# Fused attention, routing and mixture of experts: a new order of steps, memory products in row tiles, gates in a tensor of their own, more warming matmuls

## Chip, cores and metric

One core of one Trainium2 chip. The metric is the device time of one execution in microseconds (us); less is better.

## What is computed

```python
B, H, S, D = 4, 8, 576, 64
scores = causal(q @ k.T / sqrt(D));  local = softmax(scores) @ v
q_p = phi(q)                                   # elu(q) + 1
mem_out = (q_p @ M_prev) / (q_p @ z_prev + 1e-6)
g = sigmoid(beta)                              # one per head
x = concat_heads(g * mem_out + (1 - g) * local)   # 2304 tokens x 512
logits = x @ w_gate;  e = argmax(logits)          # 8 experts
gate = softmax(logits)[e] * sigmoid(x @ w_output_gate)[e]
out[t] = gate[t] * (relu(x[t] @ w1[e]) @ w2[e])   # 512 -> 1024 -> 512
```

All inputs and the output are float32.

## The kernel before

**Attention.** A pair is two heads of one batch; there are 16 pairs, each cut into five tiles of queries (128, 128, 128, 128, 64 rows). Per tile TensorE makes the scores as sums of three products of split operands, for the two heads on the two halves of the array's rows (L497; the tile of 64 rows at L484). VectorE adds the mask and takes the maximum in one pass into `st` (L555, L523), ScalarE takes the exponential (L560, L532), TensorE turns the probabilities (`pt`, L572, L541), ScalarE or VectorE copies them to SBUF (`PT`, L419), and TensorE multiplies them with the values (`po`, L607). Queries and keys arrive in one tile `qk`; a copy on ScalarE or VectorE makes its high part `hi` (L388), GpSimd the low part `lo` (L392, 1216 elements per partition). GpSimd also starts `phi` (L440), ScalarE and VectorE finish it (L444, L447).

**Memory.** For each batch and tile of queries `memory` multiplies `phi` with `mz`, which holds the matrices of two heads, their products with the gate weights and their norms, 81 columns per head (`me`, L658). VectorE then makes the norm `nr` (L664, L665), scales to `x` (L671) and sums the logits (L674). `combine` turns the attention output, weighs it on VectorE, adds it on GpSimd (`xd`, L729) and stores rows of 513 floats in the DRAM tensor `xs`: 512 of the token and one for its gate.

**Routing.** Per batch, VectorE adds the logits' parts (`lg`, L774), then takes maximum, difference `dl` (L229), one-hot `oha` (L239), `wt` (L254), and the gate `og` (L257 to L272), which SP stores into the last column of `xs` (L275). TensorE ranks the tokens per expert (`rank`), VectorE turns ranks into positions (`pcol`, L280 to L289), GpSimd makes selection matrices `selp` (L305). After the last batch two sums of small matmuls (`pp`, L977) give the row numbers of 25 slots of 128 tokens (`rowi`, L982).

**Order.** Up to the end of attention each engine's work is a list of named steps (`job`); the string `ORDER` of 1154 names sets in which order they are issued, so each engine runs its share of them in that order and waits in place. `RT1_1` is the second routing step of batch 1 (`dl`), `R9` the `lo` of pair 9, `SEL` a `selp`, `ME` a memory product; `:DVE` or `:ACT` says which of two engines copies. VectorE is DVE, ScalarE ACT, GpSimd POOL, and SyncE (SP) issues most DMAs.

**Experts.** 23 slots of up to 128 tokens run one after the other: `gather` fetches rows of `xs` (`xr`, L1033) with GpSimd's indirect DMA, `stage_x` turns and splits them (`xh`, `xl`, L1060), `gemm1` (`h`, L1083) and `gemm2` (`py`) multiply with split weights `whi`, `wlo` made from `raw` (L941, L944), `stage_h` turns and splits in between (L1106 to L1111). ScalarE scales the result by the gate, which came as element 512 of the row, and GpSimd scatters it (L1134).

**Warming.** `warm(n)` issues n matmuls of ones that nobody reads, 12 at the start, 8 and 11 in the last routing, and 11 behind `pp` (L162); their PSUM tile is one of the two buffers of tag `m` that all small products share.

## Time and profile before

| | |
|---|---|
| median of 3 runs | 526.43 us (526.43 to 528.64) |
| the profiled execution | 526.39 us, span 524.4 us |
| busy: TensorE, VectorE, ScalarE, GpSimd | 503.0, 340.9, 279.1, 291.1 us |
| largest lines of the chain that ended last | `h` 23%, `py` 22%, `pt` 7%, `po` 7%, `s` 6%, `me` 4% |
| moved | 68.22 MB, mean 130 GB/s |

The span goes from the first to the last instruction; the time of the execution is 2.0 us longer. A busy TensorE is not one at its peak, since a matmul counts as busy while it waits inside the pipeline. The chain is followed back from the last instruction, at each step to what released it. In bracketed parts of rows, "idle before" is how long the engine stood before this instruction, and what ended that.

### The profile page before, as it was taken

The numbers are of one execution on the slowest core, as the hardware profiler recorded it, in microseconds if no ns is written. First come the engines' busy times: TensorE is split into PE (matmuls) and PEld (weight loads), VectorE is DVE, ScalarE is ACT, GpSimd is POOL, SyncE is SP. The second block draws the span as 40 slices with busy tenths as digits, with TensorE's granted clock in tenths as the row PEclk, the third lists the DMA queues.
The fourth block names the chain that finished last, engine by engine and source line by source line (L and its number), as shares of the span: only waits on it lengthen the run. The fifth ranks groups of instructions, "written<-read, shape, count | busy, mean of one in ns | idle before, by whom it ended". The sixth has DMA issues, their size and how long they took to land.

```text
span 524.4 us, 10513 instructions
## 1 busy us (share of the span) xinstructions
PE 503.0 (96%) x3238; PEld 402.2 (77%) x3238; DVE 340.9 (65%) x821; ACT 279.1 (53%) x643; POOL 291.1 (56%) x264
## 2 busy tenths in 40 slices
PE   8999999999899999688999999999999999999994
PEld 4788778787777887366888888888888888888884
DVE  5998899999689988659898289500073891025600
ACT  5997788696677864353444333333444433343341
POOL 8882584676355223743577657644455675445342
PEclk9999999999699999889999999999999999999998
DMA  7632155263202513396777367511153675115000
GB/s 247 218 133 101 52 166 160 79 190 100 85 26 77 133 57 91 63 326 228 213 242 225 130 191 216 189 40 48 53 147 114 202 221 160 40 44 158 8 3 27
DMA packets 29079, 68.22 MB, mean 130 GB/s; under 512 B 6176, under 2 KB 6688, under 8 KB 29026
## 3 DMA queue, kind: packets, MB, share of 16 engines
q1 hardware_dynamic: 25186, 56.63, 35.3%
q0 software_dynamic: 3696, 10.77, 5.9%
q8 instruction: 32, 0.52, 0.4%
q14 instruction: 21, 0.17, 0.1%
q10 hardware_dynamic: 144, 0.13, 0.1%
HBM read 58.06 MB, written 10.76 MB: 131 GB/s over the span
## 4 chain that ended last, share of the span: by engine, by line
PE 84%; DVE 8%; POOL 3%; issue 3%; ACT 1%; POOLq 0%; DVEq 0%; ACTq 0%
PE h L1083 23%; PE py L1083 22%; PE pt L572 7%; PE po L607 7%; PE s L497 6%; PE me L658 4%; PE hp L1106 3%; PE sd L484 2%; DVE wlo L944 2%; PE px L1052 2%; PE pt L541 2%; PE pv L721 1%; POOL selp L305 1%; DVE st L555 1%; PE pl L824 1%
## 5 line engine op out<-in xcount | busy, mean ns | idle before, releaser
L941 DVE CAST whi<-raw 128x1024 fp32r<-128x1024 f32 x56 | 56.2, 1004 | 119.4 <-ACTq L1090 109.2
L1111 POOL TENSOR_TENSOR hl<-hT,hh 128x512 fp32r<-128x512 f32 x46 | 68.4, 1507 | 87.4 <-ACT hh L1110 87.4
L944 DVE TENSOR_TENSOR wlo<-raw,whi 128x1024 fp32r<-128x1024 f32 x63 | 95.0, 1508 | 4.0 <-ACT whi L941 1.1
L1083 PE MATMUL py<-whi,hh 128*128 (+1 forms) x192 | 77.8, 405 | 1.6 <-DVEq L947 1.6
L560 ACT ACTIVATE st<-st,nm 128x384 f32<-128x384 f32 (+3 forms) x128 | 71.2, 558 | 14.2 <-DVE nm L555 13.7
L1083 PE MATMUL py<-wlo,hh 128*128 (+1 forms) x192 | 74.2, 386 | 0.0
L1083 PE MATMUL py<-whi,hl 128*128 (+1 forms) x192 | 73.9, 385 | 0.0
L1083 PE MATMUL h<-whi,xh 128*128 (+1 forms) x184 | 73.9, 401 | 0.0
L1083 PE MATMUL h<-wlo,xh 128*128 (+1 forms) x184 | 73.0, 397 | 0.0
L1083 PE MATMUL h<-whi,xl 128*128 (+1 forms) x184 | 72.7, 395 | 0.0
L555 DVE CUSTOM_DVE_ANT_0 st<-s,mask 128x128 f32<-128x128 f32 (+3 forms) x128 | 57.9, 483 | 8.4 <-PE s L497 5.3
L1096 ACT ACTIVATE h<-h 128x1024 f32<-128x1024 f32 x23 | 23.6, 1026 | 73.4 <-PE h L1083 73.4
L392 POOL TENSOR_TENSOR lo<-qk,hi 128x1216 fp32r<-128x1216 f32 x15 | 43.1, 2870 | 27.7 <-ACT hi L388 21.3
L1110 ACT CAST hh<-hp 128x512 fp32r<-128x512 f32 x46 | 27.5, 598 | 48.7 <-PE py L1083 48.7
L419 ACT COPY PT<-pt 128x512 f32<-128x512 f32 (+2 forms) x84 | 42.1, 516 | 17.9 <-PE pt L572 14.5
L572 PE MATMUL pt<-ident,st 128*128 128x128 f32 x320 | 47.9, 281 | 3.2 <-ACT PT L419 2.4
L1060 POOL TENSOR_TENSOR xl<-x,xh 128x512 fp32r<-128x512 f32 x22 | 32.4, 1472 | 33.3 <-ACT x L1059 30.1
L1109 ACT COPY hT<-hp 128x512 f32<-128x512 f32 x46 | 27.2, 590 | 42.5 <-PE hp L1106 42.5
L607 PE MATMUL po<-PT,v 128*64 128x320 f32 (+4 forms) x480 | 47.8, 348 | 0.5 <-DVE oT L419 0.4
L572 PEld LDWEIGHTS pt<-ident,st 128*128 128x128 f32 x320 | 36.7, 143 | 9.7 <-ACT PT L419 4.1
L607 PEld LDWEIGHTS po<-PT,v 128*64 128x64 f32 x480 | 30.0, 137 | 18.4 <-issue 3.2
L1083 PEld LDWEIGHTS py<-whi,hh 128*128 128x128 f32 x192 | 36.2, 188 | 8.3 <-DVEq L947 2.2
(199 smaller groups left out, 998.6 us busy)
## 6 DMA issues: line engine op xcount, KB each, us to landing
raw<-in_w SPq DMA_DIRECT2D x64, 512.0 KB, 4.1
qk<-in_qk SPq DMA_DIRECT2D x15, 640.0 KB, 4.2
v<-in_vd SPq DMA_DIRECT2D x16, 320.0 KB, 3.8
xs<-xd SPq DMA_DIRECT2D x12, 256.0 KB, 3.5
...
```

Source lines behind the costliest of these rows:

```text
L392: G.tensor_tensor(c["lo"][:, TQ:], c["raw"][:, TQ:], f32(c["hi"])[:, TQ:], op=ALU.subtract)
L419: (A.copy if e == "ACT" else V.tensor_copy)(dst(), src())
L497: T.matmul(c()["ss", q][j], l[r, lc], m[r, KC:KC + w], start=(a == 0), stop=(a == 2))
L555: V.tensor_tensor_reduce(st[:, :w], c()["ss", qt][j], mask[:, 512 - w:512], -SCALE, 3.0e38, ALU.add, ALU.min, negm()[:, i:i + 1])
L560: A.activation(st, st, AF.Exp, bias=c()["negm"][:, i:i + 1], scale=-1.0, accum_out=sums()[:, qt, 2 * p + j:2 * p + j + 1])
L572: T.transpose(pt[:, (m * k1 + i) * P:(m * k1 + i + 1) * P], st[:, i * P:(i + 1) * P], ident)
L607: T.matmul(po[64 * j:64 * j + 64, qs - q0:q1 - q0], vt[:, k, 64 * j:64 * j + 64], PT[:, j, k, qs:q1], start=(k == 0), stop=(k == kn - 1))
L941: join((A.copy if eng is A else eng.tensor_copy)(whi[:, e % 2, c, :], raws[e, c]))
L944: join(eng.tensor_tensor(wlo[:, e % 2, c, :], raws.pop((e, c)), f32(whi[:, e % 2, c, :]), op=ALU.subtract))
L1060: G.tensor_tensor(xl, x32, f32(xh), op=ALU.subtract)
L1083: i = T.matmul(o[n % nh], l[:, z], m[:, n * 512 + part.start:n * 512 + part.stop], start=(c == 0 and k == 0 and n < nh), stop=(c == 3 and ...
L1111: G.tensor_tensor(hl[:, z], hT[:, z], f32(hh)[:, z], op=ALU.subtract)
```

## The change

The order string is replaced as a whole; the names in it are the same. Gates get a DRAM tensor `gd` of their own, and rows in `xs` are 512 floats; each slot fetches its gates with an indirect DMA of its own (`gather_gate`), right behind its row gather, but for the first three slots, where the three stand behind the last weight split ahead of the first expert product. The memory product works on 64 rows at a time, one head each, with the even heads in one PSUM tile and the odd ones in the other. From the last routing on the warming matmuls have a PSUM pool `pw` of two buffers, and the last group of them is 22 instead of 11.

```diff
--- before.py
+++ after.py
@@ -28,7 +28,6 @@
 HW = D + 16
-XW = DM + 1
...
@@ -43,62 +42,62 @@
 ORDER = """
...
-RT1_1 E10_2_1 F113 M10_2_0 E10_3_0 P9_256_0 P9_0_0 P9_256_1 O9_0:ACT T10_3_0 T10_2_1 O9_256:ACT F213 RT1_2 RT1_3 RT1_4 E10_2_0 M10_3_1 RX1 ME2_1
...
+V10_1:ACT RT1_1 G2_0 N12_3 RT1_2 OUT1_2 T9_4 N22_3 SS10_2 V9_4_0:ACT Tgate40 M10_2_0 RT1_3 M10_2_1 V9_4_1:ACT Tpos20 TS9_0 SS10_3 P9_256_0 M10_3_0
...
@@ -130,7 +129,8 @@
     dpool = ctx.enter_context(tc.tile_pool(name="dram", bufs=1, space=bass.MemoryType.DRAM))
-    xs = dpool.tile([NT + 65, XW], F32, name="xs")
+    xs = dpool.tile([NT + 65, DM], F32, name="xs")
+    gd = dpool.tile([NT + 65, 1], F32, name="gd")
     rx = ctx.enter_context(ExitStack())
@@ -156,7 +156,7 @@
     def warm(n):
-        w = psm.tile([P, 512], F32, name=f"warm{fin.setdefault('w', 0)}", tag="m")
+        w = fin.get("pw", psm).tile([P, 512], F32, name=f"warm{fin.setdefault('w', 0)}", tag="m")
         fin["w"] += 1
@@ -272,7 +272,7 @@
         def gate7():
-            SY.dma_start(xs[row(b, 0):row(b, NQ), DM:XW].rearrange("(t p) c -> p (t c)", p=P), t["og"])
+            SY.dma_start(gd[row(b, 0):row(b, NQ)].rearrange("(t p) c -> p (t c)", p=P), t["og"])
 
@@ -355,7 +355,7 @@
         b, p = divmod(g, NP)
-        c = pr[g] = {"st": {}, "pt": {}}
+        c = pr.setdefault(g, {"st": {}, "pt": {}})
         c["raw"] = (ld if g % 3 == 2 else kq).tile([P, QK], F32, name=f"qk{g}", tag="qk", bufs=1 if g % 3 == 2 else 2)
@@ -368,7 +368,7 @@
         b, p = divmod(g, NP)
-        pr[g]["vt"] = ld.tile([P, NQ, P], F32, name=f"v{g}", tag="v", bufs=3)
+        pr.setdefault(g, {"st": {}, "pt": {}})["vt"] = ld.tile([P, NQ, P], F32, name=f"v{g}", tag="v", bufs=3)
         SY.dma_start(pr[g]["vt"], vd[b, p])
@@ -643,20 +643,21 @@
         r = ROWS[qt]
-        qz = slice(TQ + qt * P, TQ + qt * P + P) if qt < NQ - 1 else slice(0, TQ)
+        qz = slice(TQ + qt * P, TQ + qt * P + P) if qt < NQ - 1 else slice(0, P)
         m = f"{b}_{qt}"
-        zs = [slice(4 * hf, 4 * hf + 4) for hf in range(2)]
+        zs = [slice(j, H, 2) for j in range(2)]
         mes = []
...
                 G.memset(t["lg"], 0.0)
-            for hf in range(2):
-                me = psm.tile([P, 324], F32, name=f"me{m}_{hf}", tag="m")
-                for pp in range(2):
-                    T.matmul(me[:r, 162 * pp:162 * pp + 162], t["phi"][2 * hf + pp][:, qz], t["mz"][:, 2 * hf + pp, :], start=True, stop=True)
-                mes.append(me[:r].rearrange("p (h c) -> p h c", c=81))
+            me = [psm.tile([P, 324], F32, name=f"me{m}_{j}", tag="m") for j in range(2)]
+            for p in range(NP):
+                for j in range(2):
+                    z = slice(64 * j, 64 * j + 64)
+                    T.matmul(me[j][:, 81 * p:81 * p + 81], t["phi"][p][z, qz], t["mz"][z, p, 81 * j:81 * j + 81], start=True, stop=True)
+            mes.extend(x[:r].rearrange("p (h c) -> p h c", c=81) for x in me)
 
@@ -674,7 +675,7 @@
         gs = range(NP * b, NP * b + NP)
-        job(f"ME{m}", "PE", 1085, due + DUE["ME"], product, after=[f"F2{g}" for g in gs] + [f"MC{b}"] + ([f"Y{b - 1}_{qt}"] if b else []) + held(due + HOLD["ME"]), takes=[("m", (m, 0)), ("m", (m, 1))], uses=[("phi", g) for g in gs] + [("mz", b)], mode="F")
+        job(f"ME{m}", "PE", 850, due + DUE["ME"], product, after=[f"F2{g}" for g in gs] + [f"MC{b}"] + ([f"Y{b - 1}_{qt}"] if b else []) + held(due + HOLD["ME"]), takes=[("m", (m, 0)), ("m", (m, 1))], uses=[("phi", g) for g in gs] + [("mz", b)], mode="R")
         job(f"N1{m}", "DVE", 460, due + DUE["N1"], norm, after=[f"ME{m}", "gates2"], takes=[("nr", m)], uses=[("m", (m, 0)), ("m", (m, 1))])
@@ -729,7 +730,7 @@
         def stored():
-            SY.dma_start(xs[row(b, qt):row(b, qt) + r, :DM], o["xd"][:r].rearrange("p h c -> p (h c)"))
+            SY.dma_start(xs[row(b, qt):row(b, qt) + r], o["xd"][:r].rearrange("p h c -> p (h c)"))
 
@@ -843,7 +844,7 @@
         def stored():
-            SY.dma_start(xs[row(b, qt):row(b, qt) + r, :DM], t["xd"][qt][:r].rearrange("p h d -> p (h d)"))
+            SY.dma_start(xs[row(b, qt):row(b, qt) + r], t["xd"][qt][:r].rearrange("p h d -> p (h d)"))
 
@@ -874,7 +875,7 @@
     constants()
-    SY.dma_start(xs[MID:MID + 1, :DM], maskd[0:1, :DM])
+    SY.dma_start(xs[MID:MID + 1], maskd[0:1, :DM])
     for b in range(B):
@@ -946,6 +947,7 @@
 
+    fin["pw"] = rx.enter_context(tc.tile_pool(name="pw", bufs=2, space=PSUM))
     warm(8)
@@ -989,7 +991,7 @@
 
-    warm(11)
+    warm(22)
     V.tensor_tensor(ge, sidx.unsqueeze(2).to_broadcast([P, NSLOT, E]), en[:, 1:].unsqueeze(1).to_broadcast([P, NSLOT, E]), op=ALU.is_ge)
@@ -1028,10 +1030,16 @@
 
+    def gather_gate(s):
+        g = st[s]["g"] = mk.tile([P, 1], F32, name=f"g{s}", tag="g", bufs=4)
+        G.indirect_dma_start(out=g, out_offset=None, in_=gd[:NT + 1], in_offset=bass.IndirectOffsetOnAxis(ap=rowi[:, s:s + 1], axis=0))
+
     def gather(s):
-        xr = mk.tile([P, XW], F32, name=f"xr{s}", tag="xr", bufs=4)
+        xr = mk.tile([P, DM], F32, name=f"xr{s}", tag="xr", bufs=4)
         G.indirect_dma_start(out=xr, out_offset=None, in_=xs[:NT + 1], in_offset=bass.IndirectOffsetOnAxis(ap=rowi[:, s:s + 1], axis=0))
         st[s] = {"x": xr, "ring": s < NMAIN}
+        if s > 2:
+            gather_gate(s)
 
@@ -1115,7 +1123,7 @@
         y = st[s]["y"] = mk.tile([P, DM], F32, name=f"y{s}", tag="y", bufs=2)
-        A.activation(y, py, AF.Copy, scale=st[s]["x"][:, DM:DM + 1])
+        A.activation(y, py, AF.Copy, scale=st[s]["g"])
         done(s, sem_2)
@@ -1123,7 +1131,7 @@
             y = mk.tile([P, 256], F32, name=f"y{s}_{n}", tag="y", bufs=2)
-            A.activation(y, py, AF.Copy, scale=st[s]["x"][:, DM:DM + 1])
+            A.activation(y, py, AF.Copy, scale=st[s]["g"])
             i = G.indirect_dma_start(out=out.rearrange("t (a d) -> (t a) d", a=2), out_offset=bass.IndirectOffsetOnAxis(ap=endi[:, n:n + 1], axis=0), in_=y, in_offset=None, bounds_check=2 * NT - 1, oob_is_err=False)
@@ -1153,6 +1161,8 @@
     ready()
+    for s in range(3):
+        gather_gate(s)
     V.tensor_copy(skip[0:1, 0:1], f32(wlo)[0:1, 0, 3, 0:1])
```

**Where instructions stand.** TensorE, the first memory product of batch 0 (`me` the product, `pt` turned probabilities, `s` and `sd` scores), before:

```order
L541 MATMUL pt_4_669<-ident,st_4_567 128x128 x4
L543 MATMUL pte_4_674<-ident,st_4_567 64x128
L658 MATMUL me_0_0_681<-mz_184,phi_223 128x162
L658 MATMUL me_0_0_681<-mz_184,phi_225 128x162
L658 MATMUL me_0_1_684<-mz_184,phi_397 128x162
L658 MATMUL me_0_1_684<-mz_184,phi_448 128x162
L572 MATMUL pt_0_0_687<-ident,st_0_0_628 128x128
```

and after the change:

```order
L497 MATMUL s_2_0_667<-hi_457 128x384
L497 MATMUL s_2_1_668<-hi_457 128x384
L659 MATMUL me_0_0_678<-mz_185,phi_268 128x81
L659 MATMUL me_0_1_679<-mz_185,phi_268 128x81
L659 MATMUL me_0_0_678<-mz_185,phi_246 128x81
L659 MATMUL me_0_1_679<-mz_185,phi_246 128x81
L659 MATMUL me_0_0_678<-mz_185,phi_343 128x81
L659 MATMUL me_0_1_679<-mz_185,phi_343 128x81
L659 MATMUL me_0_0_678<-mz_185,phi_461 128x81
L659 MATMUL me_0_1_679<-mz_185,phi_461 128x81
L484 MATMUL sd_4_0_689<-lo_458,hi_457 128x288
```

Four matmuls over all rows have become eight that alternate between the two halves, and here they stand behind scores, which also work on halves.

VectorE around `dl` of batch 1 (L229; the rows named ISA are the maxima of scores, `phi` the end of a `phi`, `nr` and `x` a memory product's norm and scaling), before:

```order
L555 ISA st_3_0_2089,nm_1928<-s_3_0_2073,mask 128x512
L555 ISA nm_1928 128x1
L229 TENSOR_TENSOR dl_2091<-lg_1310,mx_2026 128x40
L555 ISA st_2_0_2095,nm_1928<-s_2_0_2063,mask 128x384
L555 ISA nm_1928 128x1
L447 SCALAR_TENSOR_TENSOR phi_1771<-qk_1563,phi_1771 128x576
L233 SCALAR_TENSOR_TENSOR wt_2126<-dl_2091,edesc 128x40
L236 TENSOR_REDUCE mx_2026<-wt_2126 128x5
L239 SCALAR_TENSOR_TENSOR oha<-mx_2026,wt_2126 128x40
L555 ISA st_3_1_2131,nm_1928<-s_3_1_2074,mask 128x512
```

and after the change:

```order
L419 COPY oT_2072<-po_0_2051 128x256
L225 TENSOR_REDUCE mx_2074<-lg_1342 128x5
L419 COPY PT_100<-pt_0_0_2064 128x2x128
L229 TENSOR_TENSOR dl_2091<-lg_1342,mx_2074 128x40
L675 TENSOR_REDUCE lg_1883<-x_0_1927 128x16
L665 SCALAR_TENSOR_TENSOR nr_3_2094<-me_3_0_2079,gt 128x4
L665 SCALAR_TENSOR_TENSOR nr_3_2094<-me_3_1_2080,gt 128x4
L666 RECIPROCAL nr_3_2094<-nr_3_2094 128x8
L233 SCALAR_TENSOR_TENSOR wt_2098<-dl_2091,edesc 128x40
L672 TENSOR_TENSOR x_3_2108<-me_3_0_2079,nr_3_2094 128x4x80
```

`dl` has moved from between two maxima of scores to a place among a memory product's small steps.

VectorE at the end of attention (`lg` the last sums of logits, `pos` to `pcol` the positions of batch 2), before:

```order
L836 TENSOR_REDUCE lg_2730<-yl_1_3249 128x16
L836 TENSOR_REDUCE lg_2730<-yl_1_3255 128x16
L280 TENSOR_TENSOR pos_3268<-rk_3258,oha 128x40
L283 TENSOR_REDUCE ps_3269<-pos_3268 128x5
L286 TENSOR_SCALAR ohe<-ps_3269 128x5
L289 TENSOR_TENSOR pcol<-ps_3269,ohe 128x5
L811 CAST cntb<-cnt 128x8
```

and after the change:

```order
L280 TENSOR_TENSOR pos_3347<-rk_3340,oha 128x40
L283 TENSOR_REDUCE ps_3348<-pos_3347 128x5
L286 TENSOR_SCALAR ohe<-ps_3348 128x5
L289 TENSOR_TENSOR pcol<-ps_3348,ohe 128x5
L837 TENSOR_REDUCE lg_2790<-yl_1_3337 128x16
L812 CAST cntb<-cnt 128x8
L837 TENSOR_REDUCE lg_2790<-yl_1_3329 128x16
```

The two sums have moved behind the positions. GpSimd from the last selections to slot 3, after the change (before, the rows with `gd` are missing and a row of `xr` is 513 long):

```order
L305 TENSOR_SCALAR selp<-pidx,pcol,tokv 128x128 x6
L1039 DMA xr_3563<-xs,rowi 128x512
L329 MEMSET raw_0_3565 1x1
L1039 DMA xr_3570<-xs,rowi 128x512
L1039 DMA xr_3572<-xs,rowi 128x512
L945 TENSOR_TENSOR wlo<-raw_3_3219,whi 128x1024
L1035 DMA g_3598<-gd,rowi 128x1
L1035 DMA g_3600<-gd,rowi 128x1
L1035 DMA g_3602<-gd,rowi 128x1
L1068 TENSOR_TENSOR xl_3637<-x_1_3639,xh_3636 128x512
L1039 DMA xr_3692<-xs,rowi 128x512
L1035 DMA g_3694<-gd,rowi 128x1
```

The first three gate gathers stand behind the weight split of the first expert, the later ones behind their row gather. The memset waits for the store of the last gates, since its tile lies where `og` lay; the first row gather no longer does.

## Rows read from the trace of the kernel before

**Rows 1.** Busy time by stretch: start:end, length, busy of engines (instructions), TensorE clock, DMA share, GB/s.

```profile
8.00:98.00 90.00, 89.68 (x789) 71.70 (x791) 82.89 (x293) 78.85 (x223) 60.53 (x50) 1.00 0.44 148
...
125.40:132.60 7.20, 4.90 (x45) 4.02 (x41) 7.06 (x17) 4.16 (x12) 3.52 (x3) 1.00 0.21 60
132.60:142.80 10.20, 10.12 (x52) 8.64 (x52) 5.93 (x27) 6.56 (x19) 4.10 (x5) 0.50 0.19 70
...
247.10:515.00 267.90, 267.90 (x1296) 219.60 (x1297) 131.90 (x104) 103.20 (x171) 148.97 (x106) 1.00 0.43 132
```

(The engines of a row are PE, PEld, DVE, ACT, POOL, in this order.)

**Rows 2.** The chain of waits, attention: start, us, what.

```profile
70.11 0.87 PE pt L572 x8
...
86.59 1.10 PE me L658 x8
```

**Rows 3.** Timeline of GpSimd, VectorE and TensorE, and one group of VectorE's line 229.

```profile
124.64 1.56 POOL L305 TENSOR_SCALAR selp<-pidx,pcol,tokv 128x128 f16<-128x128 f16 x2
...
125.40 3.58 DVE L229 TENSOR_TENSOR dl<-lg,mx 128x40 f32<-128x40 f32 x1
...
126.17 2.75 POOL L392 TENSOR_TENSOR lo<-qk,hi 128x1216 fp32r<-128x1216 f32 x1
...
132.68 1.75 PE L572 MATMUL pt<-ident,st 128*128 128x128 f32 x7 [2.38 <-ACT PT L419]
...
L229 DVE TENSOR_TENSOR dl<-lg,mx x4: 181/196/3579, 87.1 to 209.8; 128x40 f32<-128x40 f32 x4
...
167.44 2.16 DVE L774 TENSOR_TENSOR lg<-lg,lsum 128x64 f32<-128x64 f32 x2
...
171.47 0.55 PE L572 MATMUL pt<-ident,st 128*128 128x128 f32 x3 [0.64 <-ACT st L560]
```

(The line of the group has the least, median and greatest duration in ns.)

**Rows 4.** Timeline of TensorE's weight loads, scores of 64 rows.

```profile
80.07 0.19 PEld L497 LDWEIGHTS s<-hi,lo 64*128 64x128 f32 x2
80.18 0.19 PEld L497 LDWEIGHTS s<-hi 64*128 64x128 f32 x2
```

**Rows 5.** Timeline of TensorE's matmuls, from transposes to scores.

```profile
79.08 0.60 PE L572 MATMUL pt<-ident,st 128*128 128x128 f32 x4
79.61 0.39 PE L497 MATMUL s<-lo,hi 64*128 64x256 f32 x2
```

**Rows 6.** Timeline from the last routing to the first slot; the landing of gate stores.

```profile
208.37 0.48 DVE L836 TENSOR_REDUCE lg<-yl 128x16 f32<-128x80 f32 x2
...
212.75 0.37 SPq L275 DMA_DIRECT2D xs<-og  x1
...
DMA to landing us min/median/max: 4.5/4.6/4.7
...
216.01 0.16 DVE L982 TENSOR_SCALAR rowi<-pp 128x4 int32<-128x4 f32 x1 [1.55 <-PE pp L977]
...
217.42 4.22 PE L162 MATMUL warm<-ones 128*128 128x512 bf16 x11 [0.93 <-DVE skip L988]
...
218.74 1.59 POOL L1033 DMA_INDIRECT xr<-xs,rowi  x1 [3.00 <-DVE endi L1010]
...
225.02 0.45 PE L1042 MATMUL px_x<-ident,xr 128*128 128x128 f32 x1 [3.38 <-issue]
```

**Rows 7.** The chain of waits, first expert products.

```profile
226.11 3.91 PE h L1083 x12
...
232.55 1.48 DVE wlo L944
...
261.30 5.60 PE h L1083 x24
```

**Rows 8.** GpSimd's gathers as a group; timeline of the tightest slot.

```profile
L1033 POOL DMA_INDIRECT xr<-xs,rowi x23 | 32.5, 1412 | 6.5 <-DVE endi L1010 3.0 <-issue 1.4
...
269.48 2.27 POOL L1060 TENSOR_TENSOR xl<-x,xh 128x512 fp32r<-128x512 f32 x1
...
273.89 0.39 PE L1083 MATMUL h<-whi,xl 128*128 x1
```

(A group's row has its instructions, busy us, mean ns of one, and idle time before them.)

More of the change, by code (lines that the diff above doesn't have):

```diff
@@ new lines @@
+E2_1_0 V1_4_1:ACT F13 R3 M1_3_1 M2_2_0 T2_0 gates E1_3_1 M1_3_0 E2_2_0 load5 load_v3 V2_0:DVE TS1_0 O1_0:DVE MW1 T2_1 MC1 TS0_0 SS2_4 V2_1:ACT T1_3_1
+T2_2_0 M2_2_1 E1_3_0 M2_4_0 V1_3_1:ACT SS2_3 gates2 E2_2_1 V2_2_0:DVE M2_4_1 F14 M2_3_1 M2_3_0 TS0_1 TS1_1 C4:DVE F24 T1_3_0 F23 T2_2_1 V1_3_0:ACT
+V2_2_1:ACT R4 E2_3_1 E2_3_0 E2_4 SS3_1 M3_0_0 M3_1_0 P1_256_0 T2_3_1 V2_3_1:ACT T2_3_0 P1_256_1 V2_3_0:ACT M3_1_1 E3_1_1 E3_0_0 O1_256:DVE E3_1_0 T2_4
+M3_0_1 SS3_2 V2_4_0:DVE ME0_0 E3_0_1 SS3_4 T3_0 V2_4_1:ACT M3_2_0 M3_2_1 C5:DVE R5 E3_2_1 E3_2_0 N10_0 T3_1 TS2_1 SS4_1 M3_4_0 V3_0:ACT V3_1:ACT
@@ new lines @@
+Tpos30 G2_3 R13 M10_4_0 Tpos40 E10_3_1 C14:ACT ME2_1 M10_4_1 N12_1 SS11_1 TS9_1 T10_3_0 load_v12 SS11_4 M11_0_0 N22_1 M11_1_1 M11_0_1 SEL0_3
+V10_2_0:ACT SEL0_1 T10_3_1 MW3 V10_3_0:ACT E10_4 M11_1_0 V10_3_1:ACT E11_0_1 RX1 Tgate11 RK1 E11_0_0 E11_1_1 T10_4 M11_4_0 SS11_2 E11_1_0 load12
+Tpos11 MC3 M11_4_1 TS10_1 R14 V10_4_0:DVE ME2_4 V10_4_1:DVE OUT1_4 T11_0 T11_1 M11_2_0 N12_4 E11_4 V11_0:ACT Tgate31 Tgate21 SS11_3 V11_1:ACT T11_4
+E11_2_0 F115 N22_4 GA1 M11_3_0 P11_0_0 P10_256_0 V11_4_0:DVE M11_3_1 Tpos21 F215 M11_2_1 E11_3_0 O11_0:ACT V11_4_1:ACT P10_0_0 P10_256_1 C12:ACT R12
@@ new lines @@
+E15_0_1 Tgate22 SEL1_0 M15_1_0 CB1 T15_4 E14_2_0 G3_0 O14_0:DVE W3_0 M14_2_1 E15_1_0 O13_256:ACT M15_1_1 V15_4_0:ACT PLl4_0 PLl1_0 fetch1 E15_1_1
+YLl4_0 T15_0 V15_0:ACT V15_4_1:DVE TL4_0 YLl1_0 XLl4_0 E14_2_1 GA2 PLl0_0 T14_2_0 YLl0_0 XLl0_0 W3_1_0 G3_1 CJ2 fetch2 V14_2_0:ACT T15_1 V15_1:ACT
+Tgate42 TS15_0 ME3_3 TL0_0 SS15_3 SS15_2 N13_3 T14_2_1 SEL0_4 N23_3 XLl1_0 TS15_1 V14_2_1:ACT M15_2_1 P15_0_0 O15_0:ACT M15_3_1 Tgate52 P15_512_0
+W3_1_1 TL1_0 M15_2_0 O15_512:ACT E15_2_1 M15_3_0 W3_1_4 E15_2_0 G3_3 Tgate62 fetch3 P14_256_0 P15_128_0 P14_256_1 E15_3_0 E15_3_1 T15_2_0 T15_3_0
@@ L102 @@
+O14_256:DVE O15_128:DVE PLl2_0 V15_2_0:DVE G3_2 PLl1_1 V15_3_0:ACT GO2 T15_3_1 YLl2_0 V15_3_1:ACT YLl1_1 XLl2_0 PLl4_1 TL2_0 XLl1_1 PLl3_0 TL1_1 OL1
+YLl4_1 YLl3_0 XLl4_1 TL4_1 T15_2_1 PLl0_1 YLl0_1 XLl3_0 V15_2_1:ACT W3_1_3 TL0_1 TL3_0 XLl0_1 P15_384_0 P15_256_0 W3_1_2 O15_384:ACT PLl3_1
+O15_256:ACT YLl3_1 PLl2_1 OL0 XLl3_1 YLl2_1 RK2 Tpos12 Tpos22 XLl2_1 Tpos32 Tpos42 SEL2_2 SEL2_1 SEL2_0 SEL2_4 SEL2_3 OL4 OL3 OL2 TL2_1 CB2 TL3_1
 """.split()
```

95 lines of the change are left out of this document (40 added, 55 removed).

## The prediction

> **What bounds the kernel now.** I read the busy time and granted clock by stage first. From 8.00 to 98.00 us TensorE is busy 89.68 of 90 us and VectorE 82.89 [rows 1]: attention is paced by TensorE, with VectorE at 92% close behind. TensorE's "busy" includes queueing inside its pipeline, so I checked it against the spacing of starts: eight transposes take 0.87 us of the chain, 0.109 each [rows 2], and they do run back to back. The reader should therefore expect almost any TensorE time taken out of attention to come back whole, as long as VectorE keeps up. From 247.10 us to the end TensorE is busy 267.90 of 267.90 us at full clock [rows 1]: the expert stage is bound by its own matmuls, which the change does not touch.
>
> Two stretches break the pattern. From 125.40 to 132.60 us TensorE works 4.90 of 7.20 us, and from 132.60 to 142.80 the granted clock is 0.50, the lower of its two levels [rows 1]: TensorE had idled and then ran at half speed for 10.2 us, which cost 5.1. The bridge between the attention and the expert stage (about 207 to 247 us) is a chain over VectorE, GpSimd, a gather and the first expert's matmuls.
>
> The timeline shows what caused the first stretch. VectorE's `dl` (L229), a subtraction of 40 elements with both operands in SBUF, took 3.58 us from 125.40 [rows 3], while its median over four is 196 ns. It ended at 128.98, 0.06 after GpSimd's `lo` (126.17 + 2.75 = 128.92), which had followed `selp` (from 124.64, 1.56) without a pause. So a two-operand SBUF instruction of VectorE stands still until GpSimd pauses. Everything behind it on VectorE came late, then ScalarE's copies of transposed probabilities, and TensorE waited 2.38 us for one. At 167.44 the two `lg` additions (L774) of 64 and 16 elements took 2.16 us together, and TensorE then waited 0.64 [rows 3].
>
> **The change, part by part**
>
> *Memory products in row tiles.* One of the 20 products was four program matmuls of 162 columns over 128 rows, eight in the trace, and takes 1.10 us of the chain [rows 2], 0.138 each. Now it is eight of 81 columns over 64 rows, sixteen in the trace, in pairs on the two halves of the array. The nearest rows are the scores, also pairs of 64 rows: the weight loads of two successive pairs start at 80.07 and 80.18 [rows 4], so a pair takes 0.11 whatever it multiplies, and its two loads run together. Eight pairs cost 0.88, and 20 x (1.10 - 0.88) = 4.4 us go. The lower bound of the new product is its matmuls alone, 8 x 0.138/2 = 0.55; the upper is 16 loads one after another, 1.76. I take 0.88 because the score rows have the same shape of weights.
>
> A change of tile shape costs time: four transposes start 0.109 apart from 79.08, the last at 79.41, and the score behind it starts at 79.61 [rows 5], 0.20 instead of 0.11. The order has 131 stretches of equal tile shape before the routing's end and 146 after the change, so 15 x 0.095 = 1.4 us come back. The Trainium skill (TensorEngine Tiling (Array Packing), Key Properties) says that a change of tiling mode drains TensorE, which speaks against a product that no longer shares the transposes' shape; the page has no price for it, rows 5 have 0.095 us. Net: **-3.0 us**.
>
> *The order.* All 1154 steps are the same, placed otherwise; VectorE has 54 of the 184 copies that either it or ScalarE can do, before and after. What matters is where the routing's two-operand steps stand against GpSimd's long ones. `dl` of batch 1 now stands among the norms of a memory product instead of between two score maxima, and what it delays first is that product's scaling. If the two waits that rows show go, 2.4 + 5.1 + 0.6 = 8.1 us go with them. Bounds: nothing gained (other steps collide instead) and all 8.1, plus little that is spread thinly. The order alone does not say which steps meet, and VectorE's share is still about 90%, so I keep 1.6 back for new collisions: **-6.5 us**. SP's queue is passed too: the gate stores of earlier batches now stand ahead of the last five row stores, where the one that stood among them used to hold the queue.
>
> *Gates apart.* A row is 2048 instead of 2052 bytes, a norm reads every second head: nothing for either, the element counts are the same. The first gather started at 218.74 although its row numbers were written at 216.01 + 0.16 = 216.17. The store of the last gates into the same DRAM tensor was issued at 212.75 and lands 4.5 to 4.7 us later, at 217.45 by the longest [rows 6]. From there to the gather 1.29 us are GpSimd's own start. Without that wait the gather starts 1.29 after 216.17, at 217.46: 1.28 earlier. Also, the order now takes the rank positions of batch 2 before the last two sums of `lg`, which took 0.48 [rows 6]; the selection, the slot numbers and the gather all hang on those positions. Together 1.8 us; below, nothing; above, 2.1, if GpSimd's start is partly done while it waits. The memset and the two gathers behind it still wait for the gates' store, which no longer waits for an earlier gate store and lands by then.
>
> *More warming matmuls, from PSUM of their own.* The 11 matmuls waited 0.93 us for VectorE's `skip` and took 4.22, 0.384 each, mostly at the lower clock; TensorE then idled until 225.02 [rows 6] and began the first expert product at the lower clock too: 12 matmuls took 3.91 us [rows 7], where 24 take 5.60 at full clock, 2.80 for 12. With 22 matmuls that need not wait, from 217.42 - 0.93 - 0.48 = 216.0 on, TensorE is at work for 22 x 0.384 = 8.4 us if the clock is down throughout and half of that if it is up, until 224.4 or 220.2. The first gather lands at 225.02 - 1.8 = 223.2. So the end is either in time or 1.2 late. I take a rise in between, and the 12 matmuls at full clock: 1.1 us. They are on the path: ScalarE's cast of the second expert's weights and VectorE's `wlo` at 232.55 [rows 7] come behind them, and from there VectorE's weight splitting runs to 247.1. Gather and clock: **-2.9 us**, between -0.6 and -3.2.
>
> *Gate gathers.* Each slot gets one more indirect DMA on GpSimd, at the 1412 ns of the row gathers or less [rows 8]. It stands ahead of the scatter and of `xl` of a later slot. In the tightest slot `xl` ended at 269.48 + 2.27 = 271.75, and TensorE used it at 273.89: 2.14 us of cover. A gather at its mean, with a start of 0.3, is covered by that: **0**. If the cover went, each slot that is short would cost the difference. The three that come before are issued behind GpSimd's last weight split and ahead of `xl` of slot 1, and take 3 x 1.4 of the time in which GpSimd waits for that slot's rows.
>
> **The sum.** The profiled execution took 526.39 us, the median of the runs shown is 526.43. 526.39 - 3.0 - 6.5 - 2.9 = **514.0 us**. About 0.5% (2.6 us) is what a measurement of this kernel can tell from no change.
>
> **The rivals**
>
> *A. The waits move.* The order removes these collisions and makes others of the same weight. For it: VectorE stays at about 90% while TensorE has no slack, and both waits that rows show reached TensorE. Against it: after the change the routing steps stand in clusters away from GpSimd's long instructions. Then the second term is 0, and 514.0 + 6.5 = **520.5**.
>
> *B. Slower: more episodes of a late VectorE and a fallen clock.* One wait of 3.6 us cost 2.4 of idling and 5.1 of half clock, 7.5 together. This decides by their number: with two where there was one, 526.39 - 3.0 - 2.9 + 7.5 = 528.0, within 0.5%; with three, **535.5**. For it: one such wait was enough before. Against it: of the two waits that rows show only one did it, the other cost 0.6.
>
> *C. The product halves.* If its weight loads overlap better than the scores', the product takes its matmuls' 0.55: 20 x 0.55 - 1.4 = 9.6 instead of 3.0, and 514.0 - 6.6 = **507.4**. Against it: in rows 4 the loads pace the narrow pairs. The Trainium skill (TensorEngine Tiling (Array Packing), Theoretical Speedup) gives up to two times for a contraction of 64 rows; it would be this case, and rows 4 show the loads as the nearer limit.
>
> *D. The gate gathers reach TensorE.* If one takes the 2.1 us that cover `xl` and half a microsecond more, in six slots like that one, that is 3 us: **517.0**.
>
> **How the numbers follow.** Forecast 0.55, A 0.25, B 0.10, C 0.05, D 0.05. The predicted time is that of the forecast, 514.0. Its own range is 510.5 (all 8.1 us of waits, the gather's 2.1) to 518 (half of the order's term, the gather's lower bound). The range that should hold the time takes in A with 2 us more, and leaves out B and C: 509.5 to 522.5. Faster by over 0.5% (below 523.8): the forecast, C, D and 0.18 of A, 0.83. Within 0.5%: the rest of A and B's mild form, 0.10. Slower: B's hard form, 0.07.
>
> **What would show it.** The products: 16 trace matmuls each, pairs 0.11 apart, some 0.9 us of the chain. The order: `dl`, `wt` and `lg` all near 0.2 us, no stretch of half clock between 10 us and the end of attention, attention ending some 9.5 us earlier. The gates: the first gather within 1.5 us of its row numbers. The warming: full clock when the first expert product begins, and 2.8 us for its first 12 matmuls. The expert stage: 267.9 us as before. The prediction is wrong if attention ends less than 5 us earlier, if a half-clock stretch stands in it, or if an `h` matmul waits for `xl`.

## The result, and the profile after

The changed kernel takes **534.18 us** (median; 526.71 for the kernel before beside it), ratio 1.013 with a 95% interval of 1.0097 to 1.0162. It is slower by some 7 us; the forecast was 514.0. The execution profiled took 534.79 us with a span of 533.1, against 526.39 and 524.4 before: 8.7 us of span to account for.

The stages first. The row numbers of the last routing are written at 217.96 us (before at 216.01, [rows 6]), so attention and routing lost 2 us instead of gaining 9.5. From there to the first transposes of the first expert's rows (`px_x`) it takes 11.73 us, before 9.01. From there to the first `py` it takes 16.2 us, before 14.9. The expert stage is what it was, 276.67 us from the first `py` to the last in both traces. Behind the last `py` come 10.5 us, before 7.8. So 2.0 + 2.7 + 1.3 + 2.7 us make up the 8.7. The busy time by stretch (length, then PE, PEld, DVE, ACT, POOL, the clock, DMA share, GB/s) answers to [rows 1]:

```profile
135.00:140.00 5.00, 3.51 (x39) 2.80 (x39) 4.95 (x15) 2.89 (x12) 2.61 (x1) 1.00 0.10 39
140.00:143.50 3.50, 3.50 (x16) 2.42 (x15) 2.31 (x11) 2.30 (x7) 0.00 (x0) 0.51 0.00 0
...
253.00:523.00 270.00, 269.82 (x1310) 221.45 (x1310) 134.97 (x104) 103.30 (x172) 168.33 (x125) 1.00 0.43 132
...
225.40:235.60 10.20, 5.91 (x16) 4.74 (x17) 4.17 (x8) 2.86 (x6) 8.51 (x6) 0.50 0.89 295
```

The stretch of half clock in attention is shorter (3.4 us instead of 10.2), but the bridge has one of 10.2 us. The timeline of the changed kernel shows why, and what became of the VectorE steps of [rows 3] (start, us, engine, line, operation, in brackets the idle time before and what ended it):

```profile
129.18 2.79 POOL L392 TENSOR_TENSOR lo<-qk,hi 128x1216 fp32r<-128x1216 f32 x1 [8.05 <-issue]
...
129.27 2.73 DVE L286 TENSOR_SCALAR ohe<-ps 128x5 f32<-128x5 f32 x1
...
134.82 2.79 POOL L392 TENSOR_TENSOR lo<-qk,hi 128x1216 fp32r<-128x1216 f32 x1
...
135.46 2.21 DVE L254 TENSOR_TENSOR wt<-lg,oha 128x40 f32<-128x40 f32 x1
...
154.44 0.39 SPq L275 DMA_DIRECT2D gd<-og  x1
...
166.37 1.27 POOL L730 TENSOR_TENSOR xd<-x,y 128x512 f32<-128x512 f32 x1 [4.57 <-DMA xs<-xd]
...
167.67 1.29 DVE L726 TENSOR_TENSOR y<-pv,rr 128x512 f32<-128x512 f32 x2 [1.26 <-POOL xd L730]
...
168.41 0.76 PE L607 MATMUL po<-PT,v 128*64 128x256 f32 x6 [1.16 <-DVE y L726]
...
214.94 0.37 SPq L275 DMA_DIRECT2D gd<-og  x1
...
217.96 0.16 DVE L984 TENSOR_SCALAR rowi<-pp 128x4 int32<-128x4 f32 x1 [0.78 <-PE pp L979]
...
218.29 4.91 PE L162 MATMUL warm<-ones 128*128 128x512 bf16 x22
...
219.11 1.23 POOL L1039 DMA_INDIRECT xr<-xs,rowi  x1 [1.42 <-issue]
225.24 0.09 POOL L329 MEMSET raw<- 1x1 f32 x1 [4.90 <-issue]
...
229.69 0.45 PE L1050 MATMUL px_x<-ident,xr 128*128 128x128 f32 x1 [6.49 <-issue]
```

Three things are to be read here. First, `dl` is short now, but `ohe` and `wt` are caught by GpSimd's `lo` in its place: each starts just behind a `lo` and ends 0.03 to 0.06 us after it. Second, GpSimd's `xd` stood 4.57 us until an earlier store of rows had landed, VectorE's `y` then waited 1.26 for `xd`, and TensorE 1.16 for `y`; this begins behind the gates' store of 154.44. Third, the first gather starts 1.15 us after its row numbers, as the prediction wanted, but its rows reach TensorE only 10.6 us later (before 6.3, [rows 6]), and the memset in front of the second gather, which needs the buffer that this store reads, does not run until 10.3 us after the gates' store was issued (the row names no releaser). TensorE, done with its 22 warming matmuls, idles and falls to half clock; the chain has 5.17 us for the first 12 `h`, before 3.91 [rows 7].

The view of the DMA queues from 216 to 226 us (packets, MB, their time as a share of 16 engines) says what the gather ran into:

```profile
q0 software_dynamic: 21, 0.09, 53.7%
q8 instruction: 1, 0.02, 2.1%
```

The 21 packets of the gathers kept their engines for 53.7% of 160 us, 4.1 us each, and even the fetch of program code by another queue took 3.4. The gates' store itself is 640 elements of 4 bytes, now side by side in `gd`; before they were 2052 bytes apart. The store's own packets don't show the difference. In the 2.1 us from its issue on, its queue (q1) has 656 packets of 7.4 ns each, and as many of 7.5 ns in the run with 64 bytes that comes next; only the packets of others behind it are long:

```profile
q1 hardware_dynamic: 656, 0.00, 14.5%
```

```profile
q1 hardware_dynamic: 656, 0.00, 14.6%
```

### The profile page after: what moved, and what is told of

Its sections match the earlier page's. It is cut to its first block, busy times and chain, and to the rows that moved or that the text cites. A ratio compares the mean times of both kernels' runs of the same rounds, so it can differ in the third digit from the quotient of the medians.

```text
span 533.1 us, 10897 instructions
## 1 busy us (share of the span) xinstructions
PE 502.3 (94%) x3409; PEld 398.9 (75%) x3409; DVE 346.3 (65%) x821; ACT 280.0 (53%) x643; POOL 311.8 (58%) x287
## 4 chain that ended last, share of the span: by engine, by line
PE 51%; DVE 2%; issue 2%; POOL 1%; ACT 1%; POOLq 0%; DVEq 0%; ACTq 0%
PE h L1091 23%; PE py L1091 22%; PE hp L1114 3%; DVE wlo L945 2%; PE px L1060 2%; PE warm L162 1%; DVE whi L942 1%; POOL hl L1119 0%; POOL out L1135 0%; POOL out L1142 0%; ACT whi L942 0%; PE pp L979 0%; ACT hh L1118 0%; ACT xh L1065 0%; POOLq L1213 0%
## 5 line engine op out<-in xcount | busy, mean ns | idle before, releaser
L945 DVE TENSOR_TENSOR wlo<-raw,whi 128x1024 fp32r<-128x1024 f32 x63 | 97.1, 1541 | 5.2 <-ACT whi L942 2.6
L560 ACT ACTIVATE st<-st,nm 128x384 f32<-128x384 f32 (+3 forms) x128 | 71.1, 557 | 11.1 <-DVE nm L555 10.4
L419 ACT COPY PT<-pt 128x512 f32<-128x512 f32 (+2 forms) x85 | 43.4, 525 | 20.5 <-PE pt L572 16.0
L572 PEld LDWEIGHTS pt<-ident,st 128*128 128x128 f32 x320 | 35.7, 142 | 10.1 <-ACT PT L419 3.7
L1091 PEld LDWEIGHTS py<-wlo,hh 128*128 128x128 f32 x192 | 36.1, 188 | 7.9
```

Source lines behind the costliest of these rows:

```text
L419: (A.copy if e == "ACT" else V.tensor_copy)(dst(), src())
L560: A.activation(st, st, AF.Exp, bias=c()["negm"][:, i:i + 1], scale=-1.0, accum_out=sums()[:, qt, 2 * p + j:2 * p + j + 1])
L572: T.transpose(pt[:, (m * k1 + i) * P:(m * k1 + i + 1) * P], st[:, i * P:(i + 1) * P], ident)
L945: join(eng.tensor_tensor(wlo[:, e % 2, c, :], raws.pop((e, c)), f32(whi[:, e % 2, c, :]), op=ALU.subtract))
L1091: i = T.matmul(o[n % nh], l[:, z], m[:, n * 512 + part.start:n * 512 + part.stop], start=(c == 0 and k == 0 and n < nh), stop=(c == 3 and ...
```

## The experiments

**The store of neighbouring elements.** First the distance in the changed kernel: `gd` gets 64 bytes per token. The run also has a copy that fills `gd` in the middle of attention and a VectorE step for the row numbers times 16; both add work, so neither can be what makes it faster.

```diff
-    gd = dpool.tile([NT + 65, 1], F32, name="gd")
+    gd = dpool.tile([16 * (NT + P), 1], F32, name="gd")
...
-            SY.dma_start(gd[row(b, 0):row(b, NQ)].rearrange("(t p) c -> p (t c)", p=P), t["og"])
+            SY.dma_start(gd.rearrange("(n w) c -> n (w c)", w=16)[row(b, 0):row(b, NQ), :1].rearrange("(t p) c -> p (t c)", p=P), t["og"])
...
+    V.tensor_scalar(rowg, rowi, 16.0, 0.0, op0=ALU.mult, op1=ALU.add)
```

> The changed kernel with its gates 64 bytes apart in gd instead of 4 (the gate gathers read the same 4 bytes each, from 16 times the row number); a copy that fills gd in the middle of attention is added so that every byte of it has been written. Theory S (the store of 640 neighbouring 4-byte elements is what is slow): the last gates' store lands about 4.6 us after its issue as it did in the kernel before, instead of 10.2; the memset no longer waits until 225.2 for it; the first gather, whose rows landed 10.4 us after its start, lands after 6.3 as before; the bridge shortens by 4 us plus up to 1.2 of clock, 534.2 to 529 or 530. Rival Q (the rows were late because the gather itself is slow once three gathers and a code fetch stand together): store and gather as in the changed kernel, 534. The closing drain stays 5.8 us by both.

523.52 us, ratio to the kernel before 0.9932 (0.9909 to 0.9955). The distance between the elements is worth 0.0198 of 527, **10.4 us**, more than twice what was expected, and the kernel turns from slower to faster. Its timeline and its DMA queues from 212 to 222 us (the same 10 us of the bridge):

```profile
214.22 0.16 DVE L986 TENSOR_SCALAR rowi<-pp 128x4 int32<-128x4 f32 x1 [0.77 <-PE pp L981]
...
215.37 1.23 POOL L1043 DMA_INDIRECT xr<-xs,rowi  x1 [1.42 <-issue]
216.60 0.09 POOL L329 MEMSET raw<- 1x1 f32 x1
...
221.40 0.30 PE L1054 MATMUL px_x<-ident,xr 128*128 128x128 f32 x1 [1.94 <-issue]
```

```profile
q0 software_dynamic: 80, 0.26, 14.5%
q8 instruction: 1, 0.02, 0.8%
```

80 gather packets now take 0.29 us each, where 21 took 4.1; the memset follows the gather at once; `px_x` starts 6.0 us after the gather instead of 10.6. What was missing from the expectation is that the row numbers come 3.7 us sooner as well (214.22 instead of 217.96): the earlier batches' stores had held up work within attention. From 146 to 206 us TensorE stands 4.5 us in the changed kernel (1.0 of it behind a caught `pcol`) and 0.2 with 64 bytes. GpSimd's `xd` behind the first of them, which had waited 4.57 us, now follows at once (162.15 us).

Then the reverse, in the kernel before: a store of the gates to a tensor that nobody reads, side by side and 64 bytes apart.

```diff
+            SY.dma_start(gd[row(b, 0):row(b, NQ)].rearrange("(t p) c -> p (t c)", p=P), t["og"])
```

> The kernel before with one more store per batch: the gates also go, as neighbouring 4-byte elements, into a tensor that nobody reads. Nothing waits for it but a later use of its buffer. Theory S (such a store keeps the memory busy for some 8 to 10 us, and every transfer and code fetch in that time is late): the first gather, which starts 6 us behind the last of the four stores, lands later than 6.3 us after its start, and row stores behind the first stores hold GpSimd; 529 to 535. Rival (the store was slow only because the row stores of the new order stand close to it): 526 to 527.

> The kernel before with one more store of the gates per batch, 64 bytes apart, into a tensor that nobody reads; with 4 bytes apart this made it 19 us slower. Theory S (neighbouring elements are what is slow): 526 to 528.5, the four more stores land in about 2 to 5 us. Rival (any second store of 640 elements of 4 bytes does it): 540 and above.

Side by side: **545.98 us**, ratio 1.0358 (1.0324 to 1.0392), beyond the range expected (the execution profiled took 540.78). 64 bytes apart: 526.95, ratio 1.0009 (0.9996 to 1.0022), nothing. The same number of elements, the same instruction, nobody waiting for the data: only the distance differs. In the timeline of the slow one the first gather starts 10.2 us after its row numbers, and the memset names its releaser; its queues from 227 to 237 us have the same long packets:

```profile
226.09 0.37 SPq L277 DMA_DIRECT2D gd<-og  x1
...
231.19 1.23 POOL L1035 DMA_INDIRECT xr<-xs,rowi  x1 [10.45 <-issue]
236.22 0.09 POOL L331 MEMSET raw<- 1x1 f32 x1 [3.80 <-DMA gd<-og]
...
239.57 0.45 PE L1044 MATMUL px_x<-ident,xr 128*128 128x128 f32 x1 [7.84 <-issue]
```

```profile
q0 software_dynamic: 23, 0.09, 39.0%
```

The store landed at 236.2, 10.1 us after its issue. Theory S stands for what was seen: for about 10 us behind such a store row stores, gathers and a code fetch were late, whoever issued them.

**Gates in the rows.** The changed kernel without `gd` and without gate gathers.

```diff
-    xs = dpool.tile([NT + 65, DM], F32, name="xs")
-    gd = dpool.tile([NT + 65, 1], F32, name="gd")
+    xs = dpool.tile([NT + 65, XW], F32, name="xs")
...
-        if s > 2:
-            gather_gate(s)
...
-    for s in range(3):
-        gather_gate(s)
```

> The changed kernel with the gates back in column 512 of the rows and no gate gathers; its order, its row tiles and its 22 warming matmuls stay. Theory S with theory D (the closing drain lengthens with the number of indirect DMAs, 0.12 us each for 23): the drain and the counter behind it fall from 5.80 and 1.61 us back to 3.9 and 1.15 (-2.4 us), the last store lands after 4.6 us, the first gather starts 1.3 us later after its row numbers but lands 6.3 after its start: 534.2 - 2.4 - 2.8 and up to 1.2 of clock, 528 to 529. Rival (the gates apart cost nothing and all of the loss is the order's): 534.

522.94 us, ratio 0.9921 (0.9894 to 0.9949): 5 us better than expected, for the same reason as above. Against the run with 64 bytes it differs by 0.6 us, which the intervals (about 2 us) can't tell from nothing; the profiles show two opposite things in it. With gates apart the first gather starts 1.15 us after its row numbers (here 1.93). But the end is longer: GpSimd's closing drain, which follows the last scatter (group rows of its last line, with the least, median and greatest duration in ns), in the changed kernel, here, and in a run that comes below:

```profile
L1274 POOLq DRAIN  x3: 40/108/5796, 526.4 to 532.8; - x3
```

```profile
L1266 POOLq DRAIN  x3: 40/108/3917, 515.8 to 520.3; - x3
```

```profile
L1267 POOLq DRAIN  x3: 40/107/7184, 525.8 to 533.5; - x3
```

5.80 us with gate gathers, 3.92 without, as in the kernel before; from the last `py` to the end it is 10.5 and 7.8. Whether it is the number of indirect DMAs that counts was tried in the kernel before, with 40 idle ones more:

```diff
+        for i in range(2 if s > 2 else 0):
+            g = mk.tile([P, 1], F32, name=f"g{s}_{i}", tag="g", bufs=8)
+            G.indirect_dma_start(out=g, out_offset=None, in_=xs.rearrange("n (c o) -> (n c) o", o=1)[:NT + 1], in_offset=bass.IndirectOffsetOnAxis(ap=rowi[:, s:s + 1], axis=0))
```

> The kernel before with 40 more indirect DMAs of 4 bytes a row, two behind the row gather of each slot from the fourth on, into tiles that nobody reads. Theory D (the closing drain lengthens with the number of indirect DMAs, 2.73 / 23 = 0.119 us each between the runs with gates apart and in the rows): from the last py to the end 7.84 + 4.7 = 12.6 us, the expert slots as before, 531 to 532. Rival (the drain was longer because the gates' gathers were still under way, or what it waited for was theirs alone): 7.8 us and 526 to 527. If the slots grow, the gathers reach TensorE, which is the prediction's rival D.

535.56 us, ratio 1.0165 (1.0149 to 1.0181). The drain is 7.18 us: 0.082 us more for each of the 40, and the 23 gate gathers had given 0.082 each as well. A counter ahead of the drain (INC_SWDGE_SEM) takes 1.15 us before, 1.61 with the gate gathers and 1.93 here, 0.02 each. Theory D stands, with 0.10 us for each DMA in these two. But the end grew by more: 14.0 us lie behind the last `py`, 6.2 more than before. The 2.1 us that are left GpSimd stands between its last scatter and the counter; what it waits for there is not shown. The rest, 3.2 us between first and last `py`, is the prediction's rival D: with two more gathers per slot they do reach TensorE, by the view of TensorE's waits from 240 to 520 us (us in total, times, longest; its weight loads stand 3.0 us for the same):

```profile
PE h L1086 <- POOL xl L1063: 1.7, 3, 0.7
```

With one per slot, in the changed kernel, that stretch did not grow.

**Products and order, each alone.**

> The kernel before with the memory products in row tiles and nothing else. If the products give what the prediction says, 20 x 0.22 less changes of tile shape, attention ends 3 to 4 us earlier and the time is 523 +- 1. Rival P (what they give is eaten because they shift the steps behind them into new waits, or the shape changes cost more): 526 or above.

> The kernel before with the new order of steps and nothing else (products whole, gates in the rows, 11 warming matmuls). Theory O (the order moves the waits between VectorE and GpSimd and makes more of them than it removes): attention ends 4 to 6 us later than before, 531 to 532. The prediction's rival A (moved, same weight): 526. The prediction's own term: 520. If O is wrong, the 5 us that attention lost beyond the gain of the products came from order and products together.

Products alone: 527.99, ratio 1.0028 (1.0003 to 1.0054), no gain at all. Order alone: 524.77, ratio 0.9961 (0.9947 to 0.9975), 2 us faster, which refutes theory O; a third of the prediction's 6.5.

Rival P named two ways to lose the products' gain, and the rows show the second, changes of tile shape. In the old order 19 of the 20 products stand among matmuls over all rows of the array, mostly transposes. From the first of seven transposes to the first one behind the product it takes 1.87 us before and 1.90 with the products alone (the product is cut out between the two rows):

```profile
50.24 0.93 PE L572 MATMUL pt<-ident,st 128*128 128x128 f32 x7
...
52.11 0.49 PE L572 MATMUL pt<-ident,st 128*128 128x128 f32 x3
```

```profile
50.01 0.92 PE L572 MATMUL pt<-ident,st 128*128 128x128 f32 x7
...
51.91 0.55 PE L572 MATMUL pt<-ident,st 128*128 128x128 f32 x3
```

In the new order 14 of the 20 have scores, which also work on 64 rows, on one side or both. From seven transposes to a score behind the product it takes 1.96 us with the whole product and 1.77 in row tiles (the two runs with three steps moved that come below):

```profile
52.20 0.92 PE L572 MATMUL pt<-ident,st 128*128 128x128 f32 x7
...
54.16 0.50 PE L497 MATMUL s<-lo,hi 64*128 64x512 f32 x2
```

```profile
51.15 0.93 PE L572 MATMUL pt<-ident,st 128*128 128x128 f32 x7
...
52.92 0.48 PE L497 MATMUL s<-lo,hi 64*128 64x512 f32 x2
```

Counted up to the end of attention, TensorE changes between 128 and 64 rows 58 times before, 96 times with the products alone, 64 with the order alone and 74 with both. So in the old order the changes of shape take all that the shorter products free, and VectorE is not needed to explain it. TensorE still waits there behind the same VectorE step, `dl` (3.48 us at 126.0). The execution profiled took 526.28; what makes the median 1.7 us longer is not shown.

With order and products together (the run with gates in the rows) `ohe` and `wt` are caught as in the changed kernel, at the same places, and the half clock is there too:

```profile
129.21 2.79 POOL L392 TENSOR_TENSOR lo<-qk,hi 128x1216 fp32r<-128x1216 f32 x1 [8.03 <-issue]
...
129.30 2.72 DVE L286 TENSOR_SCALAR ohe<-ps 128x5 f32<-128x5 f32 x1
...
135.49 2.23 DVE L254 TENSOR_TENSOR wt<-lg,oha 128x40 f32<-128x40 f32 x1
```

```profile
136.50:138.30 1.80, 0.42 (x7) 0.10 (x3) 1.80 (x5) 0.75 (x4) 1.16 (x1) 0.99 0.00 0
138.30:145.10 6.80, 6.80 (x35) 5.19 (x37) 4.51 (x18) 3.65 (x9) 0.00 (x0) 0.50 0.00 0
```

The Trainium skill (SBUF — State Buffer, Who interferes with whom) says that VectorE and GpSimd share one pair of SBUF ports, that whichever started first holds it for its whole instruction, and that a VectorE instruction with two SBUF inputs, or a `tensor_scalar` in its fast mode, is among those that need it. The rows agree with the first kind: `wt` has two inputs, and it ends 0.06 us behind the `lo` that ran when it started. `ohe` is a TENSOR_SCALAR with one input and is caught as well; whether it ran in that mode no row shows.

**Out of the way.** If that is the cause, keeping the caught steps apart from GpSimd's `lo` must bring the time back. Three names of the order are moved. Two are caught steps (`Tpos30`, `Tgate11`); the third, `C4`, is the copy that lets a `lo` start, and it goes behind the two `phi` steps (F24, F23) that this `lo` used to catch:

```diff
-... C4:DVE F24 T1_3_0 F23 ...
+... F24 T1_3_0 F23 C4:DVE ...
-... RT1_4 M10_3_1 F213 P9_0_0 ... Tpos30 G2_3 R13 ... RX1 Tgate11 RK1 ...
+... RT1_4 Tpos30 M10_3_1 F213 Tgate11 P9_0_0 ... G2_3 R13 ... RX1 RK1 ...
```

> The run with the gates in the rows (its order, row tiles and 22 warming matmuls), with three VectorE steps taken out of the way of GpSimd's long subtraction: C4 behind F24 and F23, Tpos30 right behind RT1_4, Tgate11 behind F213. In that run the phi step took 3.33 us at 34.1, ohe 2.72 at 129.3 and wt 2.23 at 135.5, 7.2 us more than their least, and each ended 0.06 us after GpSimd's lo. Theory C (a late VectorE step makes TensorE idle and then lose its clock): the three take 0.7, 0.15 and 0.2 us, TensorE's waits of 0.84, 0.76 and 1.55 us behind them go and so does the half clock from 138.3 to 145.1, worth 3.4: 517 to 520. Rival A (the waits move): others of the same weight appear, 522 to 524. Rival V (VectorE's time was not what TensorE ran short of): the three are short and the end comes no sooner, 522 to 523.

**517.60 us**, ratio 0.9820 (0.9792 to 0.9847), 5.3 us faster than the same kernel with the steps where they were, though every step and every cost is the same. Timeline and windows:

```profile
126.32 0.16 DVE L286 TENSOR_SCALAR ohe<-ps 128x5 f32<-128x5 f32 x1
...
127.67 0.19 DVE L254 TENSOR_TENSOR wt<-lg,oha 128x40 f32<-128x40 f32 x1
```

```profile
130.00:140.00 10.00, 9.99 (x106) 8.23 (x105) 9.87 (x38) 8.74 (x26) 6.41 (x6) 1.00 0.26 88
140.00:205.00 65.00, 62.41 (x631) 48.99 (x626) 57.51 (x223) 44.54 (x128) 33.17 (x44) 1.00 0.30 86
```

Both steps have their least duration, and the clock is full there. Theory C stands for the waits; for the clock only in part. The run with 11 warming matmuls, which comes below, is the run with the gates in the rows up to the end of attention. There `ohe` and `wt` are caught too and TensorE waits behind them as long, but the clock stays at its upper level:

```profile
128.85 2.72 DVE L286 TENSOR_SCALAR ohe<-ps 128x5 f32<-128x5 f32 x1
...
135.04 2.22 DVE L254 TENSOR_TENSOR wt<-lg,oha 128x40 f32<-128x40 f32 x1
...
137.80 1.37 PE L659 MATMUL me<-mz,phi 64*128 64x81 f32 x15 [1.37 <-DVE pos L280]
```

```profile
128.00:206.00 78.00, 74.59 (x737) 58.77 (x734) 70.59 (x258) 55.04 (x154) 38.81 (x48) 1.00 0.27 81
```

With the order alone it is the same, a wait of 1.36 us and full clock up to 206. The row numbers come at 213.67 with the gates in the rows, at 212.01 with 11 warming matmuls and at 209.09 with three steps moved. So in these profiles the waits are worth some 2.9 us, and the half clock, where it follows, some 1.7 more. Why much the same wait brings 6.8 us of half clock here, 3.4 in the changed kernel and none there is open.

> The run before this one with the memory products whole again (4 matmuls of 162 columns over 128 rows), nothing else. The prediction's term for row tiles: this one is 3 us slower than with row tiles. Theory K (what shorter products free is given back, because TensorE waits for VectorE in the same places and its clock falls there): within 1 us of it.

With whole products 520.02, ratio 0.9869 (0.9843 to 0.9895): the row tiles are worth 0.0049 of 527, **2.6 us**, once nothing gives it back. Theory K falls for this order. Two more steps (`Tpos40` behind `Tgate11`, `Tpos31` and `Tpos41` behind `Tpos21`):

> The run with three steps moved, and two more of the same kind: Tpos40 right behind Tgate11, Tpos31 and Tpos41 right behind Tpos21. In that run the two pcol steps (8 bytes of result for each of five rows, both operands in SBUF) took 1.89 us at 129.8 and 2.61 at 141.7, beside GpSimd's lo, and TensorE waited 1.23 us behind the second. Theory C: both near 0.16 us, that wait gone, 1 to 3 us faster, 515 to 516.6. Rival A: other steps are caught in their place, 517 to 518.

516.97 us, ratio 0.9827 (0.9807 to 0.9847): no further gain that can be told. Both `pcol` are short, but the next step in line is caught, and TensorE still waits 1.2 us behind it, as rival A had it:

```profile
139.54 2.47 DVE L266 TENSOR_SCALAR gw<-gw 128x5 f32<-128x5 f32 x1
```

(GpSimd's `lo` ran from 139.21 to 141.97.)

**Warming.**

> The run with the gates in the rows, with 11 warming matmuls in the last group instead of 22 (PSUM of their own as there). In that run the first h starts at 22.4 after 200 us and the first py 13.28 us later, at full clock throughout; with the order alone and 11 it was 14.56. Theory W (the 22 carry the clock up to the first expert product): the granted clock falls before the first h and the stretch is 14.0 to 14.6 us, so 0.7 to 1.3 us slower, 523.7 to 524.2. Rival (the clock holds anyway, or the 22 only delay the transposes): the same within 0.3 us or faster.

> The run before this one with 11 warming matmuls in the last group instead of 22. Where this was tried before, the stretch from the first gather's start to the first py was 20.09 us with 22 and 22.19 with 11 in the two profiles, but the medians did not differ (522.94 and 522.83), since attention had ended sooner in the second. Theory W: 1 to 2 us slower than with 22. Rival: the same within 0.5 us, since the clock falls before the first expert product with 22 as well (it did, for 3.4 us, in the run with three steps moved).

522.83 against 522.94 with 22; 518.27 against 516.97 (ratios 0.9834, 0.9813 to 0.9855, and 0.9827). Neither pair differs by more than its uncertainty. In the profiles 22 matmuls carry full clock through the first expert product in two runs (64 bytes, gates in the rows) and not in the three with steps moved: with five moved the clock is at its lower level for 3.4 us from 214.6, and with 11 for 3.4 us as well. With the gates in the rows and 11 it is there for 6.8 us from 219.1, and from the first gather's start to the first `py` it takes 22.19 us instead of 20.09; the medians agree all the same, and in that profile attention had kept full clock, as shown above. Rival and theory W are not told apart by the times; by the intervals, 22 are worth 2 us at the most.

## Why the prediction was wrong, point by point

- **The gates' store, priced at nothing.** The sentence that failed is "The memset and the two gathers behind it still wait for the gates' store, which … lands by then". The store's 4.5 to 4.7 us [rows 6] was taken over to a tensor in which its elements lie side by side, and the prediction itself noted the change of layout only for the row gather ("2048 instead of 2052 bytes"). It lands after some 10 us and makes what stands behind it late, and it cost 10.4 us (8.3 to 12.5 by the two intervals). No rival had it. This is half of the miss of 20.
- **Gate gathers: 0.** Right for the slots: 276.67 us between first and last `py` in both traces. Wrong at the end: 23 more indirect DMAs lengthened the closing drain by 1.9 us and the end by 2.7. The prediction counted them against the slots' cover alone and put nothing down for the program's end.
- **The order: -6.5, measured -2.1 alone.** `dl` is 0.2 us as forecast and its 10.2 us of half clock went, but `ohe`, `wt`, `pcol` and a `phi` step were caught instead. Rival A described it, with too little weight at 0.25. Alone, the order also pays for whole products beside scores (1.96 us instead of 1.87 in the rows above), which the whole change does not. The prediction's argument against rival A, that the routing steps "stand in clusters away from GpSimd's long instructions", was read from the order where only a time could tell. Of its mechanism, a late VectorE step that starves TensorE and then its clock, the first half is right: moving three names gave 5.3 us. The second half, 5.1 us of half clock behind one wait, is no fixed price: waits of 1.35 to 1.38 us had 6.8, 3.4 and no us of it behind them.
- **Memory products: -3.0, measured -2.6** between the two runs with steps moved; 16 matmuls in pairs 0.11 apart, as forecast. The 2.6 are uncertain by 2, and they compare with whole products in the new order, which are dearer than in the old one. From the last matmul in front of a product to the first behind it, 19 of the 20 take 23.8 us before, 25.4 whole in the new order and 21.9 in row tiles there (without the one that waits or runs at half clock). So of the 3.0 the rows show 1.9. Alone it was +1.5 (0.2 to 2.8), against "almost any TensorE time taken out of attention" comes back: in the old order there was none to take out. The prediction had the kind of this price right (15 changes of shape more) and counted it for both parts together; that the products need the new order it did not say.
- **The bridge: -2.9.** Right: the first gather starts 1.15 us after its row numbers. Wrong: full clock at the first expert product, since the gather landed 4.3 us late. With 64 bytes `px_x` comes 7.2 us after the row numbers, before 9.0. But with the order alone, gates in the rows, it is 7.9 already, so the gates' own tensor gave some 0.7 of the 1.8. The warming's 1.1 isn't shown in the medians.
- **The sum by ratios** (of 527): order -2.1, products and warming on top of it -2.1, gates apart +0.6, neighbouring elements +10.4. Each is the step from one run to the next, so they add up to the measured +6.8 by construction; all but the first are uncertain by about 2. Against the forecast's -6.5, -4.1 (products and the warming's 1.1), -1.8 and 0 this is 4.4, 2.0, 2.4 and 10.4 too much, together the 19.2 between -12.4 and +6.8.
- **Rivals.** C (the product halves): no, 2.6 us. B, the slower case, named another mechanism than the one that made it slower: half clock in attention fell from 10.2 to 3.4 us in the profiles.
